# A block mask as extra contraction rows of the score matmuls, in a fused attention and MLP kernel

## The chip, the cores and the metric

The kernel runs on one core of a Trainium2 chip. The metric is the device time of one execution in microseconds, the median of several. The engines have these names in the profile: PE is TensorE's matmul stream, PEld its weight loads, DVE is VectorE, ACT is ScalarE, POOL is GpSimd. In these traces an instruction that waits holds back those behind it on its engine: in the kernel before, VectorE waits 16.5 us for beta, and its first cast, which needs no beta, starts right behind, at 21.18 us.

Ratios are computed as the mean time of one kernel's fast runs over that of the other's fast runs of the same rounds, so they are not quite the ratios of the medians quoted beside them.

## The reference

```python
# attention: batch 4, 8 heads, 768 positions, head width 64, blocks of 32
scores = q @ k.T / sqrt(64)
mask = (neighbouring blocks) | (first and last block, row or column) | (3 sampled blocks per block row)
scores = where(mask, scores, -1e9)
x = softmax(scores) @ v                     # [3072 tokens, 512]
# MLP: d_model 512, d_ff 2048
h = x @ w_in
out = (h * sigmoid(beta * h)) @ w_out
```

The mask is made of 24 by 24 blocks, so the 768 by 768 matrix has rank 24 at most. That is what the change uses.

## The kernel before

Two heads form a pair; there are 16 pairs, four per batch. `emit_prep` casts k, q and v of a pair to fp16, transposes k and q on PE and copies them to `kT` and `qT`: head 0 in partitions 0 to 63, head 1 in 64 to 127. An attention step takes a chunk of 128 keys, multiplies both heads' scores into one PSUM tile, takes the exp on ScalarE and multiplies by the 0/1 mask on VectorE.

```python
def emit_mask():                       # the mask, expanded to [128, 6, 768] in SBUF
    ...                                # maskx = block mask x one-hot, [24, 768]
    for lo, hi in ((0, 256), (256, S)):
        for c in range(NC):            # 12 matmuls and 12 evictions on VectorE
            nc.tensor.matmul(ps[:, 0:hi - lo], lhsT=oh_flat[:, c * P:(c + 1) * P],
                             rhs=maskx[:, lo:hi], start=True, stop=True)
            nc.vector.tensor_copy(out=mask_sb[:, c, lo:hi], in_=ps[:, 0:hi - lo])
# --- an attention step ---
for i in range(kn):
    for hh in range(2):                # 64 rows each: head 0 below, head 1 above
        nc.tensor.matmul(sc[:, hh, i * n:(i + 1) * n],
                         lhsT=kT[hh * D:(hh + 1) * D, ...], rhs=qT[hh * D:(hh + 1) * D, ...], ...)
nc.scalar.activation(out=et, in_=sc, func=AF.Exp, bias=0.0, scale=SCALE)
for hh in range(2):
    nc.vector.tensor_tensor(out=et[:, hh], in0=et[:, hh], in1=mask_sb[...], op=ALU.mult)
```

After that `av` multiplies `et` with v and a column of ones, VectorE scales by the reciprocal of the sum (`recip`, `xst`), PE transposes (`xtp`) into `xT_sb`. The MLP then runs `hp` (w_in), tanh on ScalarE, `g` on VectorE, and `op` (w_out). The work goes in seven groups of query tiles: the MLP of one group is interleaved with the attention of the next. The first group is attention only, for 256 queries of four pairs, and there is no MLP to fill its gaps. I call the time until the first `hp` the start, and the rest the steady stage. beta is read with one 4-byte element per descriptor, and the weights are loaded through GpSimd's DMA queue, from 2.55 us on.

The softmax here doesn't subtract the row's maximum and nothing guards it: scores larger than these inputs give would overflow.

## Time and profile before

| | before |
|---|---|
| time, median of 3 first runs | 352.86 us (351.29 to 353.05) |
| span of the profiled run | 351.1 us |
| first `hp` | 60.59 us |
| first `hp` to the end | 290.5 us |
| VectorE busy | 250.6 us, of it 108.9 in mask products |

The page of the kernel before. The first line after the span is busy time and share; then 40 slices of the span with the busy share in tenths; then groups of instructions with their total, the mean of one, and the idle time before them with its cause.

```profile
span 351.1 us, 6634 instructions
...
PE 302.9 (86%) x2670; PEld 152.1 (43%) x2670; DVE 250.6 (71%) x666; ACT 216.4 (62%) x281; POOL 9.7 (3%) x26
...
PE   0029788989998999978999989999999999999995
...
DVE  0059898998799774699976698655998456973460
...
L218 DVE TENSOR_TENSOR et<-et,mask_sb 128x512 f16<-128x512 f16 x288 | 108.9, 420 | 30.6 <-ACT et L215 28.5
...
L209 PE MATMUL sc<-qT,kT 64*128 64x256 f16 (+1 forms) x384 | 63.1, 351 | 11.0 <-ACT et L215 8.0
...
L209 PEld LDWEIGHTS <-kT 64*128 64x128 f16 x384 | 18.5, 97 | 54.8 <-issue 48.5
```

PE does nothing in the first two slices (17.6 us), VectorE next to nothing, and PE stands at two and seven tenths in slices 3 and 5. From slice 6 to the last but one it is at eight or nine tenths, but for one slice. VectorE's mask products are its largest item, but PE sets the pace.

The list of waits of the kernel before: who waited for whom, total, times, longest.

```profile
PEld L209 <- issue: 48.5, 102, 1.4
...
DVE beta_h_sb L135 <- DMA beta_sb<-in_moe_beta_dram: 16.5, 1, 16.5
```

The timeline of PE of the kernel before, at the first `hp` and in the steady stage: start, length, instruction, how many in a row.

```profile
60.59 1.47 PE L273 MATMUL hp<-xT_sb,w_in_sb 128*128 128x256 f16 x12
...
200.54 0.39 PE L209 MATMUL sc<-qT,kT 64*128 64x512 f16 x2
200.87 1.04 PE L273 MATMUL hp<-xT_sb,w_in_sb 128*128 128x512 f16 x4
201.84 0.39 PE L209 MATMUL sc<-qT,kT 64*128 64x512 f16 x2
202.16 1.90 PE L273 MATMUL hp<-xT_sb,w_in_sb 128*128 128x512 f16 x8
```

Two `sc` matmuls together last 0.39 us, as long as one alone: the heads run side by side. The single start times behind the last lines, worked out from the same trace (start in us, then ns since the previous start), show what that costs at its edges:

```
203.463  +216  hp
203.679  +216  hp
203.990  +311  sc, head 0        <- 95 more than 216
203.994    +4  sc, head 1
204.444  +450  sc, head 0        (waited for an sc buffer)
204.450    +6  sc, head 1
204.769  +319  hp                <- 103 more than 216
```

311 and 319 ns are also the medians of the steady stage at N = 512, so an entry to the 64-row mode costs about 95 ns here and an exit about 103. The Trainium skill names a drain there, without a number ("TensorEngine Tiling (Array Packing)", Key Properties: "Changing tiling mode (not just tile) drains the TensorE").

The windows view of the kernel before for the steady stage: stretch, length, then busy time and count of PE, PEld, DVE, ACT, POOL, then clock, DMA share, GB/s.

```profile
60.60:351.10 290.50, 272.18 (x2426) 134.35 (x2424) 214.57 (x561) 195.46 (x260) 0.00 (x0) 1.00 0.17 55
```

### The profile page before, as it was taken

What the parts mean: (1) busy time and instruction counts of PE and PEld (TensorE: products, weight loads), DVE (VectorE), ACT (ScalarE), POOL (GpSimd) and SP (SyncE); (2) the same over time, 40 slices, a digit from 0 to 9 for tenths busy, and PEclk for the clock granted to TensorE, in tenths of its full rate; (3) what the DMA queues carried; (4) which work ended last, traced back from release to release, by engine and by line L of the source; (5) the groups of instructions that cost most, each with busy time, mean ns of one, the idle gap of its engine ahead of it and who ended that gap; (6) DMA issues with size and microseconds to landing.
All of it is one profiled execution on the core that took longest, in us unless ns stands there. A gap on an engine that the chain in (4) does not pass through costs nothing.

```text
span 351.1 us, 6634 instructions
## 1 busy us (share of the span) xinstructions
PE 302.9 (86%) x2670; PEld 152.1 (43%) x2670; DVE 250.6 (71%) x666; ACT 216.4 (62%) x281; POOL 9.7 (3%) x26
## 2 busy tenths in 40 slices
PE   0029788989998999978999989999999999999995
PEld 0013464654443544444545344444344444444562
DVE  0059898998799774699976698655998456973460
ACT  1003649995598565788455798645986655964361
POOL 9100000000000000000000000000000000000000
PEclk9999998999999999999999999999999999999999
DMA  7999971027321422011431000001000011001101
GB/s 207 259 224 268 314 222 64 2 91 251 127 90 47 131 85 101 33 47 56 126 121 60 32 1 2 30 32 54 8 2 1 33 44 48 0 2 59 48 16 60
DMA packets 22914, 29.79 MB, mean 85 GB/s; under 512 B 3428, under 2 KB 19812, under 8 KB 22884
## 3 DMA queue, kind: packets, MB, share of 16 engines
q1 hardware_dynamic: 16512, 25.17, 21.9%
q0 software_dynamic: 4224, 4.19, 7.1%
q10 hardware_dynamic: 2148, 0.01, 0.4%
q8 instruction: 21, 0.34, 0.4%
q14 instruction: 9, 0.07, 0.1%
HBM read 27.27 MB, written 6.29 MB: 96 GB/s over the span
## 4 chain that ended last, share of the span: by engine, by line
PE 61%; ACT 16%; DVE 11%; DMA 7%; issue 4%; ACTq 0%
PE op L292 20%; PE hp L273 16%; ACT et L215 11%; PE av L239 9%; PE sc L209 8%; DMA beta_sb<-in_moe_beta_dram 5%; ACT t_sb L278 4%; DVE et L218 4%; PE tp L185 4%; DVE g L280 3%; PE xtp L253 3%; DVE xst L245 2%; DMA vst<-in_v_dram 2%; PE mk L166 1%; DVE recip L244 0%
## 5 line engine op out<-in xcount | busy, mean ns | idle before, releaser
L215 ACT ACTIVATE et<-sc 128x1024 f16<-128x1024 f32 x144 | 143.1, 1033 | 86.4 <-PE sc L209 85.3
L218 DVE TENSOR_TENSOR et<-et,mask_sb 128x512 f16<-128x512 f16 x288 | 108.9, 420 | 30.6 <-ACT et L215 28.5
L292 PE MATMUL op<-w_out_sb,g 128*128 128x512 f16 x384 | 97.4, 380 | 0.0
L273 PE MATMUL hp<-xT_sb,w_in_sb 128*128 128x512 f16 (+1 forms) x448 | 94.0, 349 | 0.8 <-DVE g L280 0.2
L278 ACT ACTIVATE t_sb<-hp,beta_h_sb 128x512 f16<-128x512 f32 (+1 forms) x112 | 69.4, 640 | 16.5 <-PE hp L273 16.2
L280 DVE SCALAR_TENSOR_TENSOR g<-t_sb,hp 128x512 f16<-128x512 f16 (+1 forms) x112 | 67.1, 608 | 8.7 <-ACT t_sb L278 7.6
L209 PE MATMUL sc<-qT,kT 64*128 64x256 f16 (+1 forms) x384 | 63.1, 351 | 11.0 <-ACT et L215 8.0
L239 PEld LDWEIGHTS <-et 128*128 128x128 f16 x1152 | 45.2, 100 | 27.2 <-DVE xst L245 14.8
L273 PEld LDWEIGHTS <-w_in_sb 128*128 128x128 f16 x448 | 39.9, 97 | 36.1 <-issue 8.4
L292 PEld LDWEIGHTS <-g 128*128 128x128 f16 x384 | 31.7, 97 | 34.3 <-issue 8.2
L209 PEld LDWEIGHTS <-kT 64*128 64x128 f16 x384 | 18.5, 97 | 54.8 <-issue 48.5
L297 ACT ACTIVATE osb<-op 128x512 f32<-128x512 f32 x24 | 14.4, 599 | 25.7 <-PE op L292 25.7
L244 DVE RECIPROCAL recip<-av 128x2 f32<-128x2 f32 (+1 forms) x64 | 11.1, 173 | 20.3 <-PE av L239 20.1
L245 DVE TENSOR_TENSOR xst<-av,recip 128x128 f16<-128x128 f32 (+1 forms) x64 | 22.7, 355 | 1.1
L185 PE MATMUL tp<-identity,k_152 128*128 128x128 f16 x6 | 0.8, 310 | 21.8 <-DVE k_152 L180 21.8
L255 DVE COPY xT_sb<-xtp 128x256 f16<-128x256 f16 (+1 forms) x32 | 11.4, 356 | 8.2 <-PE xtp L253 8.1
L253 PE MATMUL xtp<-identity,xst 128*128 128x128 f16 x96 | 11.2, 227 | 3.6 <-DVE xst L245 3.4
L135 DVE TENSOR_SCALAR beta_h_sb<-beta_sb 128x16 f32<-128x16 f32 x1 | 0.2, 174 | 16.5 <-DMA beta_sb<-in_moe_beta_dram 16.5
L253 PEld LDWEIGHTS <-xst 128*128 128x128 f16 x96 | 5.9, 98 | 12.6 <-DVE xst L245 11.4
L239 PE MATMUL av<-va_73,et 128*128 128x65 f16 x216 | 9.9, 199 | 1.2 <-DVE xst L245 1.0
L239 PE MATMUL av<-va_77,et 128*128 128x65 f16 x216 | 9.3, 196 | 1.8 <-DVE xst L245 1.8
L239 PE MATMUL av<-va_79,et 128*128 128x65 f16 x216 | 9.9, 199 | 0.7 <-DVE xst L245 0.5
(140 smaller groups left out, 128.1 us busy)
## 6 DMA issues: line engine op xcount, KB each, us to landing
kst<-in_k_dram SPq DMA_DIRECT2D x16, 384.0 KB, 3.3
qst<-in_q_dram SPq DMA_DIRECT2D x16, 384.0 KB, 4.6
vst<-in_v_dram SPq DMA_DIRECT2D x16, 384.0 KB, 4.7
out_dram<-osb SPq DMA_DIRECT2D x24, 256.0 KB, 2.0
w_in_sb<-in_moe_w_in_dram POOLq DMA_DIRECT2D x4, 512.0 KB, 15.4
w_out_sb<-in_moe_w_out_dram POOLq DMA_DIRECT2D x4, 512.0 KB, 27.3
sb_i_96<-in_sampled_blocks_dram ACTq DMA_DIRECT2D x1, 0.3 KB
beta_sb<-in_moe_beta_dram ACTq DMA_DIRECT2D x1, 8.0 KB, 18.8
```

The lines of the kernel that those rows point to most:

```text
L185: nc.tensor.transpose(out=tp[:, c, :], in_=st16[:, c, :, :].rearrange("p h d -> p (h d)"), identity=identity)
L209: nc.tensor.matmul(sc[:, hh, i * n:(i + 1) * n], lhsT=kT[hh * D:(hh + 1) * D, (kc0 + i) * P:(kc0 + i + 1) * P], rhs=qT[hh * D:(hh + 1) * D ...
L215: nc.scalar.activation(out=et.rearrange("p h i n -> p h (i n)"), in_=sc, func=AF.Exp, bias=0.0, scale=SCALE)
L218: nc.vector.tensor_tensor(out=et[:, hh], in0=et[:, hh], in1=mask_sb[:, kc0:kc0 + kn, q0:q0 + n], op=ALU.mult)
L239: nc.tensor.matmul(av[:, qc, :], lhsT=et[:, hh, i, qc * P:(qc + 1) * P], rhs=va[:, hh, kc, 0:D + 1], start=(kc == 0), stop=(kc == NC - 1))
L245: nc.vector.tensor_tensor(out=xstage[:, 0:nq, hh * D:(hh + 1) * D], in0=av[:, 0:nq, 0:D], in1=recip[:, 0:nq].to_broadcast([P, nq, D]), op= ...
L253: nc.tensor.transpose(out=xtp[:, qc, :], in_=xstage[:, qc, :], identity=identity)
L273: nc.tensor.matmul(hp[:, 0:n], lhsT=w_in_sb[:, c, f * P:(f + 1) * P], rhs=xT_sb[:, c, t0:t0 + n], start=(c == 0), stop=(c == NPAIR - 1))
L278: nc.scalar.activation(out=t_sb[:, 0:n], in_=hp[:, 0:n], func=AF.Tanh, bias=0.0, scale=beta_h_sb[:, f:f + 1])
L280: nc.vector.scalar_tensor_tensor(out=g[:, f, 0:n], in0=t_sb[:, 0:n], scalar=1.0, in1=hp[:, 0:n], op0=ALU.add, op1=ALU.mult)
L292: nc.tensor.matmul(op, lhsT=g[:, f, ts * P:(ts + 1) * P], rhs=w_out_sb[:, f, :], start=(f == 0), stop=(f == N_FFC - 1))
L297: nc.scalar.activation(out=osb, in_=op, func=AF.Copy, bias=0.0, scale=0.5)
```

## The change

The score of a key and a query gets the mask added inside the matmul. The contraction is extended by 24 rows: the one-hot block number of the key on one side, and, on the other, the row of the block mask of the query, with 0 where allowed and -30000 where not. After the exp a masked score is 0, so the product on VectorE goes. Head 0 contracts 64 + 24 = 88 rows; head 1, whose data sit in partitions 64 to 127, contracts all 128, with rows 24 to 63 filled with zeros. So the heads no longer run side by side, and PE stays in one mode. Besides, beta is read as 16 rows and transposed on PE, the weight loads wait until pair 3's k has landed (counting from 0), the mask is built ahead of the first pair's preparation, and `et` has 14 buffers instead of 16. The cut below is shortened; its lines on beta are in words.

```diff
+    def gate(w, like):
+        nc.gpsimd.tensor_copy(out=w[0:1, 0, 0:1], in_=like[0:1, 0, 0:1])
...
+    for i in range(NSET):                       # 5 sets of kA, qA, kB, qB
+        nc.gpsimd.memset(four["kB"][0:D, :], 0.0)
+        nc.gpsimd.memset(four["qB"][0:D, :], 0.0)
...
+    def emit_set(i):
+        nc.vector.tensor_copy(out=four["qA"][D:D + NB, :], in_=maskx)
+        nc.gpsimd.tensor_copy(out=four["kA"][D:D + NB, :], in_=oh_flat)
+        nc.vector.tensor_copy(out=four["qB"][0:NB, :], in_=maskx)
+        nc.gpsimd.tensor_copy(out=four["kB"][0:NB, :], in_=oh_flat)
...
-            nc.vector.tensor_copy(out=xT, in_=tp.rearrange("p c s -> p (c s)"))
+            nc.vector.tensor_copy(out=four[f"{name}A"][0:D, :], in_=flat[0:D, :])
+            nc.vector.tensor_copy(out=four[f"{name}B"][D:P, :], in_=flat[D:P, :])
...
+                kx, qx = (four["kA"], four["qA"]) if hh == 0 else (four["kB"], four["qB"])
+                rows = D + NB if hh == 0 else P
+                    nc.tensor.matmul(sc[:, i * n:(i + 1) * n], lhsT=kx[0:rows, ...], rhs=qx[0:rows, ...])
...
-                for hh in range(2):
-                    nc.vector.tensor_tensor(out=et[:, hh], in0=et[:, hh], in1=mask_sb[...], op=ALU.mult)
...
-    beta_sb = [P, N_FFC], read "(c p) -> p c"
+    beta_sb = [N_FFC, P], read "(c p) -> c p", then nc.tensor.transpose
...
     def prep_upto(i):
...
+                if n_loaded[0] == 3:
+                    gate(w_in_sb, loaded[seq[3]][0])
+                    for i in range(4): emit_w_in(i)
+                    for i in range(4): emit_w_out(i)
```

## The prediction

> **What bounds the kernel now.** Two stages.
>
> Start (0 to 60.8 us). VectorE's in-order queue waits 16.5 us (list of waits) for beta, whose small packets land 18.8 us after issue; its first conversion starts at 21.2 us (timeline). Building the mask then holds PE and VectorE until 36 us. The first `hp` matmul is at 60.8 us (chain).
>
> Steady state (60.8 to 351 us). PE is 92 to 98% busy in the windows. Start to start, `hp` and `op` at N=512 take 216 ns, `av` about 32. The two heads' `sc` matmuls (64 rows each) start 3 to 4 ns apart, so they run side by side, as the Trainium skill says ("TensorE: Matmul & The Clock Gate", Part 3). But from `hp` to the `sc` pair it is 311 ns and from the pair to the next `hp` 318 to 320, not 216: some 100 ns lost at each change. The skill names this ("TensorEngine Tiling (Array Packing)", Key Properties: changing tiling mode drains the engine); this trace agrees. I sum PE's needs here to 210.6 us without `sc`, 30.2 for `sc` pairs, 21.7 for 224 mode changes, 23.5 of waits (on ACT freeing `sc`, on VectorE for `et` and `xst`), 4 of tail.
>
> **What the change does.**
> - Removes 288 mask products (108.9 of VectorE's 250.6 us) and 12 mask evictions (6 us).
> - Removes the mode changes, and with them the side-by-side heads. An isolated N=512 pair costs 311+318-216 = about 415 ns; two full-row matmuls cost 432. So PE gains nothing by itself: steady `sc` goes from 51.9 to about 57.1 us (estimate from these spacings).
> - Adds 32 PSUM copies on VectorE (0.47 us each, 15 us) and 10 mask-row copies (5 us at most): net busy 155 to 170 us.
> - ACT: the same exp elements in 160 instead of 144 instructions; within 3 us.
> - Start: beta is read in 16 rows and transposed; weights no longer compete with the first pairs' loads. GpSimd gets 10 memsets and 10 copies (0.7 to 0.9 us each, estimated from the onehot lines), most copies behind eight weight issues of 0.77 us, so pair 1's scores wait until about 22 us. VectorE then bounds the first group: some 25 us of queued work after the mask at about 12 us.
>
> **Critical path.** First `hp` at about 39 instead of 60.8 us (gain about 21). Steady: 210.6 + 57.1 + 13 waits + 4 tail = 285 instead of 290 (the waits on mask products go, `sc` costs 5 more). Of 109 us off VectorE only some 10 are on the path there. Weights (25 us of DMA-engine share) should land in time, w_out barely.
>
> **Predicted time: 326 us**, range 313 to 339. Chances: faster by over 2% 0.94, within 2% 0.05, slower 0.01.
>
> **What would show it.** Right: first `hp` at 36 to 43 us; spacing at `sc` 216 (N=512) and 109 ns, the 100 ns steps gone; PE above 92% in steady windows; VectorE busy near 160; ACT near 215. Wrong: `sc` spacing above 230 ns (88 against 128 rows still draining); `hp` or `op` waiting on weight DMA between 40 and 70 us; first `hp` after 48 us.
>
> **What would make it wrong.** GpSimd copies much slower than 0.9 us or held by the gate, delaying group 0; weights late; ACT, at two thirds, becoming the new wait for `sc` buffers so that the steady stage does not shorten; or, the other way, waits vanishing altogether (about 313).

## The result, and the profile after

| | before | after |
|---|---|---|
| time, median of 4 | 352.30 us | 339.32 us (339.28 to 339.46) |
| ratio | | 0.9634 (0.9605 to 0.9663) |
| first `hp` | 60.59 us | 52.70 us |
| first `hp` to the end | 290.5 us | 284.7 us |
| VectorE busy | 250.6 us | 181.7 us |

It is faster by 13 us. The prediction said 26 and a range that ended at 339; the median lies 0.3 us outside. The split shows where: the steady stage was predicted as 285 us and took 284.7; the first `hp` was predicted at about 39 us and came at 52.7. The whole miss is in the start.

The page of the changed kernel:

```profile
span 337.4 us, 6399 instructions
...
PE 298.4 (88%) x2659; PEld 172.2 (51%) x2659; DVE 181.7 (54%) x408; ACT 215.8 (64%) x297; POOL 28.0 (8%) x48
...
PE   0055589999999999999999999999999999999995
...
DVE  3989764543787451557866366115667114561360
```

The waits of the changed kernel: the 48.5 us before score weight loads are 6.7, and PE waits 10.3 us for the block mask at the start.

```profile
PE mkx L180 <- DVE mask_121 L126: 10.3, 1, 10.3
...
PEld L234 <- issue: 6.7, 17, 0.9
```

The timeline of PE of the changed kernel, at the mask matmul, at the first `hp` and in the steady stage. From the `sc` at 203.56 to the `hp` at 203.77 it is 0.21 us: the steps of 100 ns are gone.

```profile
17.35 0.81 PE L180 MATMUL mkx<-onehot,mask_121 24*24 24x512 f16 x2 [10.26 <-DVE mask_121 L126]
...
52.70 1.47 PE L294 MATMUL hp<-xT_sb,w_in_sb 128*128 128x256 f16 x11
...
203.56 0.38 PE L234 MATMUL sc<-qB_163,kB_162 128*128 128x512 f16 x1
203.77 1.03 PE L294 MATMUL hp<-xT_sb,w_in_sb 128*128 128x512 f16 x4
```

The windows view of the changed kernel, the steady stage:

```profile
52.70:337.40 284.70, 274.74 (x2438) 154.94 (x2435) 142.29 (x325) 199.15 (x277) 0.00 (x0) 1.00 0.15 52
```

VectorE lost 72 us here (214.57 to 142.29), and the stage became 5.8 us shorter: its limit is PE.

The timeline of VectorE and GpSimd of the changed kernel in the start is where the surprise sits:

```profile
4.43 1.05 DVE L204 CAST k_192<-kst 128x768 f16<-128x768 f32 x1
...
6.16 0.73 POOL L166 MEMSET kB_144<- 64x768 f16 x1
...
6.80 3.90 DVE L204 CAST q_203<-qst 128x768 f16<-128x768 f32 x1 [1.31 <-DMA qst<-in_q_dram]
...
6.83 0.73 POOL L167 MEMSET qB_145<- 64x768 f16 x1
...
7.51 0.73 POOL L166 MEMSET kB_150<- 64x768 f16 x1
8.19 0.73 POOL L167 MEMSET qB_151<- 64x768 f16 x1
8.87 0.73 POOL L166 MEMSET kB_156<- 64x768 f16 x1
9.55 0.73 POOL L167 MEMSET qB_157<- 64x768 f16 x1
10.23 1.13 POOL L166 MEMSET kB_162<- 64x768 f16 x1
10.62 1.17 DVE L217 CAST va_70<-vst 128x768 f16<-128x768 f32 x1
...
11.70 1.17 DVE L204 CAST k_234<-kst 128x768 f16<-128x768 f32 x1
...
14.37 0.54 DVE L204 CAST q_245<-qst 128x768 f16<-128x768 f32 x1
...
23.69 0.83 POOL L190 COPY kB_150<-onehot 24x768 f16<-24x768 f16 x1
23.86 0.55 DVE L213 COPY kA_142<-tp 64x768 f16<-64x768 f16 x1
```

The same cast of 128 by 768 takes 0.54 us when GpSimd is quiet and 1.05, 1.17 and 3.90 us while GpSimd runs its fills. GpSimd is held up too: its last two fills take 1.13 and 1.14 us instead of 0.73, and its last copy, beside three casts, 2.24 instead of 0.8 us. VectorE's busy time counts the blocked time as work, so the share of busy time does not betray it; the length of one instruction does.

### The profile page after: what moved, and what is told of

Same layout as the page of the kernel before. It is cut to its first block, busy times and chain, and to the rows that moved or that the text cites. A ratio compares the mean times of both kernels' runs of the same rounds, so it can differ in the third digit from the quotient of the medians.

```text
span 337.4 us, 6399 instructions
## 1 busy us (share of the span) xinstructions
PE 298.4 (88%) x2659; PEld 172.2 (51%) x2659; DVE 181.7 (54%) x408; ACT 215.8 (64%) x297; POOL 28.0 (8%) x48
## 4 chain that ended last, share of the span: by engine, by line
PE 64%; DVE 16%; ACT 14%; issue 4%; DMA 2%; SPq 0%; ACTq 0%; DVEq 0%
PE op L313 23%; PE hp L294 16%; PE sc L234 12%; PE av L260 9%; ACT et L240 8%; ACT t_sb L299 6%; DVE g L301 4%; PE tp L209 2%; PE xtp L274 2%; DMA qst<-in_q_dram 2%; DVE q_203 L204 1%; DVE va_70 L217 0%; DVE xst L266 0%; DVE qB_157 L214 0%; DVE qB_139 L214 0%
## 5 line engine op out<-in xcount | busy, mean ns | idle before, releaser
L240 ACT ACTIVATE et<-sc 128x1024 f16<-128x1024 f32 (+1 forms) x160 | 146.8, 953 | 80.4 <-PE sc L234 80.2
L294 PE MATMUL hp<-xT_sb,w_in_sb 128*128 128x512 f16 (+1 forms) x448 | 95.6, 348 | 1.0 <-DVE g L301 0.2
L294 PEld LDWEIGHTS <-w_in_sb 128*128 128x128 f16 x448 | 42.2, 97 | 35.9 <-issue 1.9
L260 PEld LDWEIGHTS <-et 128*128 128x128 f16 x1152 | 44.2, 99 | 21.6 <-DVE xst L266 10.4
L313 PEld LDWEIGHTS <-g 128*128 128x128 f16 x384 | 34.9, 97 | 33.2 <-DVE qB_163 L214 0.4
L260 PE MATMUL av<-va_70,et 128*128 128x65 f16 x216 | 9.6, 199 | 2.8 <-DVE xst L266 2.7
L234 PE MATMUL sc<-qB_139,kB_138 128*128 128x256 f16 (+1 forms) x48 | 11.6, 344 | 0.5 <-ACT et L240 0.5
L234 PE MATMUL sc<-qA_137,kA_136 88*128 88x256 f16 (+1 forms) x48 | 11.1, 344 | 0.5 <-ACT et L240 0.3
L180 PE MATMUL mkx<-onehot,mask_121 24*24 24x512 f16 (+1 forms) x2 | 0.8, 506 | 10.3 <-DVE mask_121 L126 10.3
L260 PE MATMUL av<-va_72,et 128*128 128x65 f16 x216 | 9.5, 196 | 0.0
L234 PE MATMUL sc<-qB_145,kB_144 128*128 128x256 f16 (+1 forms) x36 | 8.8, 348 | 0.9 <-ACT et L240 0.9
L234 PE MATMUL sc<-qA_143,kA_142 88*128 88x256 f16 (+1 forms) x36 | 8.7, 350 | 0.6 <-ACT et L240 0.6
L234 PE MATMUL sc<-qB_163,kB_162 128*128 128x512 f16 (+1 forms) x36 | 8.5, 325 | 0.7 <-ACT et L240 0.7
```

The costliest lines, as they stand in the source:

```text
L234: nc.tensor.matmul(sc[:, i * n:(i + 1) * n], lhsT=kx[0:rows, (kc0 + i) * P:(kc0 + i + 1) * P], rhs=qx[0:rows, q0:q0 + n], start=True, stop ...
L240: nc.scalar.activation(out=et[:, 0:kn * n], in_=sc[:, 0:kn * n], func=AF.Exp, bias=0.0, scale=SCALE)
L260: nc.tensor.matmul(av[:, qc, :], lhsT=et[:, i * n + qc * P:i * n + (qc + 1) * P], rhs=va[:, hh, kc, 0:D + 1], start=(kc == 0), stop=(kc == ...
L294: nc.tensor.matmul(hp[:, 0:n], lhsT=w_in_sb[:, c, f * P:(f + 1) * P], rhs=xT_sb[:, c, t0:t0 + n], start=(c == 0), stop=(c == NPAIR - 1))
L313: nc.tensor.matmul(op, lhsT=g[:, f, ts * P:(ts + 1) * P], rhs=w_out_sb[:, f, :], start=(f == 0), stop=(f == N_FFC - 1))
```

## The experiments

Two theories for the late start. A: the new fills and copies on GpSimd block VectorE's casts. B: the order of the queues delays the first group. Rivals for the whole: the products themselves were on the path, or the beta and weight loads made all of the gain. The first four experiments ran together on one chip, the next four on another; each is compared with the kernel before in its own rounds. The last ran alone, later, on the first chip, and the record lists for it the seven earlier runs of the kernel before and one new one.

All readings in one table. "mkx" is the start of the mask matmul; it, the first `hp` and the rest come from the profiled run. The border at the first `hp` moves with the work: 316 score matmuls stand behind it in the kernel before, 326 in e3, 327 in the changed kernel (216 ns each at N = 512 in full rows), so the split into start and rest is good to about 2 us.

| kernel | mkx, us | first `hp`, us | rest, us | median time, us | ratio to before |
|---|---|---|---|---|---|
| before | 27.13 | 60.59 | 290.5 | 352.3 to 353.3 | 1 |
| after | 17.35 | 52.70 | 284.7 | 339.32 | 0.9634 |
| e1_act_fill | 12.84 | 44.95 | 284.1 | 330.13 | 0.9346 (0.9323 to 0.9368) |
| e2_unshadow | 17.42 | 52.72 | 284.7 | 339.46 | 0.9617 (0.9594 to 0.9639) |
| e3_no_product (wrong result) | 27.34 | 54.04 | 282.6 | 339.21 | 0.9616 (0.9572 to 0.9661) |
| e4_beta_only | 16.92 | 51.98 | 290.4 | 344.88 | 0.9780 (0.9721 to 0.9840) |
| e5_beta_gate | 14.03 | 47.71 | 290.5 | 338.73 | 0.9601 (0.9555 to 0.9647) |
| e6_half_rows (wrong result) | 17.56 | 56.81 | 298.7 | 360.29 | 1.0205 (1.0152 to 1.0257) |
| e7_order | 12.70 | 43.59 | 283.6 | 328.98 | 0.9325 (0.9283 to 0.9367) |
| e8_best | 8.43 | 39.69 | 286.1 | 327.67 | 0.9290 (0.9260 to 0.9321) |
| e9_onehot_first | 7.18 | 38.61 | 285.6 | 326.73 | 0.9236 (0.9198 to 0.9273) |

### e1_act_fill: the fills and one-hot copies on ScalarE

```diff
-        nc.gpsimd.memset(four["kB"][0:D, :], 0.0)        # and qB
+        nc.scalar.activation(out=four["kB"][0:D, :], in_=identity[0:D, 0:1].to_broadcast([D, S]),
+                             func=AF.Copy, bias=0.0, scale=0.0)
-        nc.gpsimd.tensor_copy(out=four["kA"][D:D + NB, :], in_=oh_flat)      # and kB
+        nc.scalar.copy(out=four["kA"][D:D + NB, :], in_=oh_flat)
```

The weight loads were pinned behind the gate in GpSimd's queue, since three of them would have moved ahead of it now that GpSimd is free early.

> The changed kernel with its ten zero fills and ten one-hot copies moved from GpSimd to ScalarE, which is idle in the first 22 us; the weights stay behind the same gate. Theory A (GpSimd and VectorE block each other in the start): VectorE's first eight casts take about 0.55 us each instead of up to 3.9, the mask matmul comes at 12.5 to 14 us instead of 17.35, the first hp at 45 to 49 us instead of 52.7, and the time is 332 to 336 us. Theory B (only the order of VectorE's and PE's queues holds the first group back, or the loads do): the casts may shorten, but the first hp stays within 2 us of 52.7 and the time is 337.5 to 340.

The page's busy times, the timeline of VectorE and PE of this kernel, and the windows views of the start, of the changed kernel first and then of this one:

```profile
PE 297.1 (90%) x2659; PEld 171.4 (52%) x2659; DVE 173.9 (53%) x408; ACT 231.0 (70%) x317; POOL 10.2 (3%) x28
```

```profile
4.41 0.54 DVE L206 CAST k<-kst 128x768 f16<-128x768 f32 x1
...
6.07 0.56 DVE L206 CAST q<-qst 128x768 f16<-128x768 f32 x1 [1.12 <-DMA qst<-in_q_dram]
...
8.27 0.56 DVE L219 CAST va<-vst 128x768 f16<-128x768 f32 x1 [1.64 <-DMA vst<-in_v_dram]
...
12.84 0.81 PE L182 MATMUL mkx<-onehot,mask 24*24 24x512 f16 x2 [4.41 <-DVE mask L126]
```

```profile
0.00:17.35 17.35, 0.26 (x1) 0.18 (x2) 11.35 (x18) 1.28 (x1) 16.33 (x36) 1.00 0.90 313
17.35:52.70 35.35, 23.45 (x224) 17.07 (x225) 28.05 (x65) 15.36 (x20) 11.66 (x13) 1.00 1.16 270
...
0.00:12.84 12.84, 0.26 (x1) 0.18 (x2) 5.09 (x18) 10.14 (x13) 3.77 (x19) 1.00 0.86 280
12.84:44.95 32.11, 22.40 (x224) 16.31 (x225) 26.59 (x65) 22.10 (x29) 6.48 (x9) 1.00 1.16 278
```

Theory A holds, with more than it promised: 330.1 us against an expected 332 to 336. The q cast takes 0.56 us instead of 3.90, the mask matmul comes 4.5 us earlier and the first `hp` 7.75 us earlier. The loads are the same, and the order of VectorE's queue is the same but for two small moves. VectorE's busy time falls from 181.7 to 173.9 us with the same 408 instructions, so 7.8 us of what the profile called work was waiting. That this equals the gain at the first `hp` is chance: 6.3 us of it lie before the mask matmul (11.35 to 5.09), which came 4.5 us earlier, and 1.5 after it (28.05 to 26.59), where 3.2 us were gained. The other 1.8 us there are not assigned: the one-hot copies also come earlier, and PE's queue has another order (in e1 the transposes of the third and of the fourth pair stand ahead of the first pair's second head, in the changed kernel the third's alone).

### e2_unshadow: the order of the preparations

The change reuses a name: the counter of the weight loads overwrites the argument `i` of `prep_upto`, so a call for pair 1 goes on to pair 3.

```diff
-                    for i in range(4): emit_w_in(i)        # i is also prep_upto's argument
+                    for wc in range(4): emit_w_in(wc)      # the same for emit_w_out
```

> The changed kernel with one name changed: the loop counter of the weight loads no longer overwrites the argument i of the function that prepares pairs, so the call that should prepare up to pair 1 no longer goes on to pair 3. Theory B (queue order): the first reciprocal comes at 29 to 32 us instead of 35.4, the first hp at 46 to 50 us instead of 52.7, time 333 to 337. Theory A (contention alone): first hp within 1.5 us of 52.7, time 338 to 340.

The first reciprocal did come at 31.4 us instead of 35.4, as theory B said. But the first `hp` stayed at 52.72 and the time at 339.46. Theory B in this form falls: advancing pair 0 alone moved nothing. That three more pairs have to pass before the first `hp` is the likely reason; no run tests it. The slip in the name costs nothing here.

### e3_no_product: the kernel before without its mask products

```diff
-                for hh in range(2):
-                    nc.vector.tensor_tensor(out=et[:, hh], in0=et[:, hh], in1=mask_sb[...], op=ALU.mult)
```

> The kernel before without its 288 mask products, so the result is wrong on purpose; PE's work is unchanged, with heads side by side and mode changes. My theory (VectorE's products are on the path only through waits of some 9 us in the steady stage and about 2 us per pair in the first group): steady stage 280 to 283 instead of 290.5 us, time 335 to 342. Rival (the 109 us off VectorE are what counts, and the full-row scores give part of it back): time under 330.

The windows view of this kernel, the steady stage:

```profile
54.04:336.70 282.66, 269.93 (x2436) 134.16 (x2434) 129.22 (x303) 198.12 (x265) 0.00 (x0) 1.00 0.16 52
```

The products of 108.9 us busy were worth 7.9 us in the steady stage (290.5 to 282.6) and 6.5 in the start. With heads side by side and mode changes, the stage takes 282.6 us here; with full rows it takes 284.7. So the stage with full rows is 2.1 us longer than with the old form without its products. The full-row form is not what brings the gain; it is the price of removing the products, and a small one.

### e4_beta_only and e5_beta_gate: the two small parts on their own

```diff
+  e4: beta read as 16 rows and transposed on PE; mask still a product
+  e5: the same, and the weight loads behind pair 3's k
```

> The kernel before with only the beta load changed (16 rows, turned on PE). If the beta wait alone held the start: first conversion at about 5 us, first hp at 46 to 52 us instead of 60.6, steady stage unchanged at 290, time 338 to 344. If the loads and the mask hold it just as much, which I hold likelier since the weights share the DMA engines until about 53 us: first hp at 53 to 58, time 345 to 350.

> The kernel before with the beta load changed and the weight loads gated on pair 3's k, the mask still a product. If keeping the weights off the DMA engines is worth something, the first pairs' loads end earlier and the first hp comes at 45 to 49 us instead of the 52.0 of the beta change alone, time 338 to 342. If the loads were not what holds the first group (VectorE is), first hp 50 to 53 us and time 343 to 346. Steady stage 290 in both.

The new beta load alone brings the first `hp` to 52.0 us; e4's time, 344.88, lies between the two ranges expected and its first `hp` at the edge of the first. Gating the weights brings it to 47.7, so holding them back while the first pairs arrive is worth another 4.3 us. The steady stage does not move. Together these two lines make the kernel as fast (338.7 us) as the whole change did (339.3); the intervals of the two ratios overlap. So, as it was written, the mask in the matmul added nothing on top: it gained 5.8 us in the steady stage and lost 5.0 in the start (47.7 to 52.7). With e1's fix it adds 8.6 us (338.7 to 330.1; two chips, each against the kernel before).

### e6_half_rows: what the mode changes cost

```diff
-                rows = D + NB if hh == 0 else P         # lhsT=kx[0:rows], rhs=qx[0:rows]
+                r0 = hh * D                             # lhsT=kx[r0:r0 + D], rhs=qx[r0:r0 + D]
```

> The changed kernel with its score matmuls cut back to the 64 rows of the head, so the mask is not applied and the result is wrong on purpose; one head per step still, so no two heads run side by side. Theory (entering and leaving the 64-row mode costs some 97 ns each time): about 200 mode changes, 19 to 22 us, come back in the steady stage, which goes from 284.7 to 300 to 308 us; time 354 to 362. Rival (the 100 ns belong to pairing the heads, or to waits, not to the mode): time within 2 us of 339.

The windows view and the timeline of PE of this kernel, the steady stage:

```profile
56.81:355.50 298.69, 289.47 (x2424) 140.24 (x2422) 143.09 (x325) 197.48 (x271) 0.00 (x0) 1.00 0.14 47
```

```profile
199.74 0.38 PE L294 MATMUL hp<-xT_sb,w_in_sb 128*128 128x512 f16 x1
200.06 0.60 PE L234 MATMUL sc<-qB,kB 64*128 64x512 f16 x2
200.59 1.04 PE L294 MATMUL hp<-xT_sb,w_in_sb 128*128 128x512 f16 x4
```

From `hp` to `sc` it is 0.32 us again, and from the first `sc` of two to the next `hp` 0.53 instead of 0.43. Between the first `hp` and the end, 224 changes of mode stand in the trace, and the start-to-start times at them sum to 22.0 us above those of full-rate matmuls, 98 ns each. The stage is only 14.0 us longer than the changed kernel's (298.7 against 284.7): 13 of its score matmuls (2.8 us) went into the start, which is 4.1 us longer, and all other gaps sum to 8.0 us instead of 13.3. Ten matmuls of the stage still ran beside one of the other head, which the expectation had excluded; the 1.8 us that this saved are counted in the 8.0. The time, 360.3 us, is in the range expected, but the stage is 1.3 us below its own. Contracting fewer rows is slower here: in the changed kernel the matmuls of 88 and 128 rows start 215 to 220 ns apart at N = 512 (medians), like full ones; it is the mode that costs.

### e7_order, e8_best, e9_onehot_first: what else holds the start

e7 adds to e1 an issue order in the first group: the preparation of pair x behind the scores of pair x-2 on PE and behind the scaling of pair x-3 on VectorE.

```diff
+                if 2 <= x <= 5: behind.enter_context(tc.issue_after(last_sc[x - 2]))
+                if 3 <= x <= 6: behind.enter_context(tc.issue_after(last_xst[x - 3]))
                 emit_prep(*seq[x])
```

> The kernel with the fills on ScalarE (330.1 us, first hp at 44.95) with the counter's name mended and, besides, the preparation of pair x put behind the scores of pair x-2 on PE and behind the last scaling of pair x-3 on VectorE. Theory B in its second form (PE's in-order queue holds pairs' scores behind later pairs' transposes, so the first group's scores pile up at the end): first hp at 40 to 42.5 us, time 325 to 328. Rival (VectorE's total work of the first group sets the end whatever the order): first hp 44 to 46, time 329 to 331.5.

The first `hp` came at 43.6 us, 1.4 earlier than in e1, between the two ranges; the time, 328.98, is nearer the rival's. The ratios' intervals of e1 and e7 overlap, so the order is worth little. The windows view of e7 from the mask matmul to the first `hp`:

```profile
12.70:43.59 30.89, 23.53 (x229) 15.95 (x230) 25.92 (x64) 23.92 (x31) 6.51 (x9) 1.00 1.16 277
```

VectorE works 25.9 us of these 30.9: about the amount of work that I predicted (25 us), but not without gaps.

e8 takes work off VectorE and starts it earlier.

```diff
+    onehot, maskx: 64 rows high; their rows 24 to 63 are zero by construction, so no fills
+    the block mask ahead of the first casts on VectorE; beta's transpose after pair 0's
+    the B half of the k and q copies of the first five pairs on ScalarE
```

> A version meant to be better: the previous one, with the one-hot table 64 rows high so that its own zero rows replace all ten fills, the mask chain ahead of the first casts on VectorE, beta's transpose moved behind the first pair's, and the second head's half of the k and q copies of the first five pairs on ScalarE. If VectorE's work and its late start bound the first group: mask matmul at 6.5 to 8 us, first hp at 33 to 38 us, steady stage 284, time 319 to 324. If the loads or the weights bound it instead: first hp after 39 us, or hp waiting for weights, time 326 to 331.

The mask matmul came at 8.4 us (6.5 to 8 expected) and the first `hp` at 39.7; the time is 327.7 us, so the last two fall in the second expectation's ranges. But its reason, loads or weights, is not seen: no wait for a load longer than the 5.0 us for the sampled blocks stands before the first `hp` on PE, VectorE or ScalarE. ScalarE had become the busy engine of the first group (27.7 of 31.3 us from the mask matmul to the first `hp`; VectorE 23.3), with pairs 6.3 us apart by its one-hot copies. The first `hp` is 3.9 us earlier than e7's but the time only 1.3 us shorter: 8 more score matmuls (1.7 us at 216 ns) lie behind it, so the start alone overstates a gain.

e9 makes the one-hot copies at once, before the pairs:

```diff
+        nc.scalar.copy(out=four["kA"][D:D + NB, :], in_=oh_flat[0:NB, :])   # in the set-up loop, all five sets
+        nc.scalar.copy(out=four["kB"][0:D, :], in_=oh_flat)
```

> The version of 327.7 us with its ten one-hot copies made by ScalarE as soon as the table exists (4.5 to 12.8 us), not one pair at a time. In that version ScalarE has 6.2 us of work per pair in the first group (four exps of 0.75, four copies of 0.8) and pairs come 6.3 us apart. If ScalarE's work sets that pace: pairs 4.6 to 5.2 us apart, first hp at 34 to 37 us, time 322 to 325.5. If the dependence of each pair's preparation on the pairs before sets it: still about 6 us apart, first hp 38 to 40, time 326.5 to 328.5.

326.7 us and a first `hp` at 38.6: the second theory's ranges. The pairs' last reciprocals come at 23.5, 29.2, 34.2 and 37.3 us, so the spacing is 5.7, 5.0 and 3.2 us, against 6.6, 6.4 and 3.7 in e8; ScalarE's load seems to have been part of it. What else sets it I did not separate. e9 is correct and beats both kernels: 0.9236 of the kernel before.

## Why the prediction was right or wrong

- "Steady: 210.6 + 57.1 + 13 waits + 4 tail = 285": right. Measured 284.7 us. Summing PE's needs in the same way over the changed kernel's trace gives about 266 us of matmul spacing, 14 us of waits and 4 of tail.
- "Removes the mode changes, and with them the side-by-side heads. PE gains nothing by itself": right. The spacing at `sc` is 216 and 109 ns, e6 shows what the changes cost, and e3 against the changed kernel shows the two forms 2.1 us apart.
- "Of 109 us off VectorE only some 10 are on the path there": right in kind; e3 measured 7.9 us.
- "First hp at about 39 instead of 60.8 us (gain about 21)": this is the step that failed: the mask was to come at about 12 us and VectorE's queue to take 25 more; the mask came at 17.35 and the first `hp` 35.4 us behind it, at 52.7, a gain of 7.9. Of the missing 13.7 us, e1 shows 7.75 to come from the fills and copies on GpSimd: 4.5 us before the mask matmul (17.35 against 12.84), where VectorE's blocked casts are the cause, and 3.2 after it (35.4 against 32.1 us from there to the first `hp`), of which VectorE's longer instructions make up 1.5. I had counted the GpSimd instructions at their own durations, and for eight of ten fills (0.73 us) and eight of ten copies (0.81 to 0.84 us) rightly. I had not counted what they do to another engine's instructions.
- "VectorE then bounds the first group: some 25 us of queued work after the mask at about 12 us": with the blocking away, the mask comes at 12.8 us and VectorE has 26.6 us of work, near the predicted 25, but the group takes 32.1 us (e1), since VectorE is idle for 5.5 us, 4.5 of it in waits for PE (its list of waits). The order of the queues accounts for 1.4 us of the delay (e7). Taking a queue's sum for a stage's length assumed no gaps. The remaining 4 to 5 us are not assigned to one cause.
- "VectorE busy near 160": wrong, 181.7; 7.8 of it is blocked time (e1). Most of the rest is an error of arithmetic: the products cover 108.9 us, but in the records other VectorE instructions overlap 14.1 us of these. The others alone cover 155.9 us of the kernel before, and taking the products out lowered the busy time by 94.1 us (250.6 to 156.5 in e3), not by 108.9.
- The warnings named GpSimd copies "much slower than 0.9 us or held by the gate" and late weights. Neither made the miss: eight of the ten copies took 0.8 us (the others 1.03 and 2.24, beside casts); the last eight did stand behind the gate and the weight issues until 21.05 us, as the prediction had counted in; and no wait of `hp` or `op` for a weight DMA stands in the list. The danger was the reverse one, VectorE slow because of GpSimd.

The skill would have warned me: "SBUF — State Buffer", Who interferes with whom, says that VectorE copies and casts in a two-port mode and GpSimd instructions share one pair of ports, and that the loser "fully blocks". This trace agrees (0.54 against 1.05 to 3.90 us), though no view names the mode that a cast ran in. Copies from PSUM were spared: at 23.86 us, with a GpSimd copy running, one took 0.55 us.

## What to carry to other kernels

Before giving "idle" GpSimd a dozen fills and copies, ask which VectorE instructions run at that time: here casts (up to 3.90 instead of 0.56 us) and copies within SBUF (up to 0.88 instead of 0.35 us) stood still while GpSimd filled and copied, and the profile shows the stop as busy time, visible only as one instruction longer than its twins. Here a third of VectorE's work in the steady stage went away and the stage became 5.8 us shorter: what counts are the waits that the limiting engine had on it. Find those in the window where the limiting engine idles, and cost the new form on the limiting engine by start-to-start spacing, edges included. When a change has several parts, run the small ones alone: here the beta load and the gate alone made as much as the whole change, until the fills were moved.

## What the Trainium skill lacked or had wrong

- "SBUF — State Buffer", Who interferes with whom, says that whoever issues first gets the shared ports. A cast that began at 6.80 us, while a fill was running, then lost to five further fills as well, which began at 6.83, 7.51, 8.19, 8.87 and 9.55 us; the cast ended at 10.70. So the blocked side can lose several times in a row, 3.90 us instead of 0.56, which the page doesn't say.
- "TensorEngine Tiling (Array Packing)", Key Properties, names the drain at a change of tiling mode but gives no number. Here a change cost 95 ns on entry and 103 ns on exit (medians), beside 216 ns for a matmul of 512 columns. Performance Considerations on that page gives row tiling for contractions of up to 64 without weighing this: with two heads side by side and full-row work between, the gain and the cost nearly cancelled (about 415 against 432 ns per pair at N = 512).
- "Perfetto Trace Analysis", Identifying the Most-Contended Engine, judges VectorE, ScalarE and GpSimd by occupancy. It does not say there that VectorE's occupancy includes the time blocked by GpSimd: 181.7 against 173.9 us for the same 408 instructions.
